# P in one two-head tile per fill, attention's output in six shared 4 KB tiles, X in three tiles

## The chip, the cores and the metric

The kernel runs on one core of one Trainium2 chip. The core has a matrix engine (TensorE, shown as PE, its weight loads as PEld), a vector engine (DVE), a scalar engine (ACT), GpSimd (POOL) and a queue engine (SP). They run side by side and wait for each other by semaphores. The metric is the device time of one execution in microseconds, and the median of several is compared. The profile calls the time from the first to the last instruction the span.

## The reference

One sequence of 2048 tokens with 640 features goes through two branches, and a gate mixes them. All is float32.

```python
def A(x):                                   # attention in 4 segments of 512 tokens, 32 heads of 20
    q, k, v = x @ wq, x @ wk, x @ wv        # each cut into heads and segments
    M, z = 0, 0
    for s in range(4):
        p = softmax(q[s] @ k[s].T * 20**-0.5 + causal_mask)
        a_dot = p @ v[s]
        a_mem = (phi(q[s]) @ M) / (phi(q[s]) @ z + 1e-6)   # phi(t) = t + 1 if t > 0 else exp(t)
        out[s] = g * a_mem + (1 - g) * a_dot               # g = sigmoid(beta), one per head
        M += phi(k[s]).T @ v[s];  z += phi(k[s]).sum()
    return out @ wo
def B(x): return (silu(x @ w1) * (x @ w3)) @ w2            # 1728 hidden features
gate = sigmoid((x * gate_w).sum(-1))
result = gate * A(x) + (1 - gate) * B(x)
```

## The kernel before

Features lie on the 128 partitions and tokens along the free dimension, so X of a segment is five blocks (kb 0 to 4) of 128 x 512. A factor of the large products is kept as a high and a low part (`split`, `split_psum`), and three passes (`PASSES`) are added in one PSUM bank: 15 matmuls of 512 columns make a block of 128 output features (`proj`). This makes q, k, the two FFN products g and u (all at L267), v (L398), the FFN's second product f (L593) and the output projection op (L852).

Attention runs in quads m of four heads (two pairs, k = 0 and 1, of two heads, i = 0 and 1). `s_fill` computes logits for the row maxima, which DVE takes (L654). `max_rows` turns the maxima round (tile `mr`) and sends them to two rows of the q tile `qk` by two transfers of ACT's queue (L670). `t_fill` then computes transposed logits in five fills of two banks, one bank for each i; a fill packs blocks (k, kb) at column o by the table `T_FILL`. ACT takes the exponential into P (L688), POOL zeroes what lies above the diagonal (`affine_select`, L693), and `pv_quad` multiplies P with V for four heads at once (L703). DVE copies the result to `oq`, from where it goes to DRAM as `od`. A visit to a quad stands at two places among the other matmuls: s0 t0 t1 o t3 s2 t2 s1 in the large one, s3 t4 s4 in the small one, where t and o belong to earlier quads (`VISITS`).

Three memories are of concern here. P is one tile of 2 x 1280 columns for a pair (10 KB in a partition; the table `PSEG` says where each kb lies), in three buffers that the first weights (`w01s`, `wr`) use too. `big_tile` is one buffer of 10.5 KB that holds in turn the raw weights `wr01`, the feature maps phi(q) of segments 1 and 2 (`pq`), the high part of segment 0's output (`oT`), X of segment 2 as loaded (`xr2`), and the memory's output `gm`. `oall` is one of 10 KB for attention's output as loaded from `od`, later its low part. The memory states `Ms` have ten tiles of 672 bytes. X has two buffers of 20 KB.

At a segment's end `o_load(c, b)` brings block b of attention's output from `od` (SP's queue, several pieces for a block), `load_memory(c)` the memory's output from `gd` (POOL's queue), and `normalize(c)` scales and adds both (rr, gt) and splits the sum for `oproj(c)`. For segment 1 `o_load` runs at about 610, 630 and 661 us, `load_memory` at 665 us, `normalize` at 690 us. `memory_read(2)`, the last to read `pq2`, ends at 664 us.

PE's instructions stand in the order in which the code writes them. The order on the other engines is made by the scheduler from its own estimate of times; `here` keeps an instruction in the written order. A transfer of SP or ACT takes one of eight semaphores (DMAHW0 to 7) in turn, and is not issued before the transfer that used the same semaphore last has landed; POOL's transfers do the same with eight of their own.

Of the kernel before, what the change touches and what calls it, by code (L numbers as in the profile page):

```python
# [17 lines left out]
P = 128  # L18
# [10 lines left out]
NP, AGE = 3, 4  # L29
# [5 lines left out]
PSEG = ((0, 512), (512, 384), (1024, 256), (896, 128))  # L35
# [3 lines left out]
def gated_mix(ctx: ExitStack, tc: tile.TileContext, xT, w01, wqk, wv, w13, w2, w2h, wo, beta, out):  # L39
# [27 lines left out]

    def constants():
# [6 lines left out]
        one = cp.tile([P, KB, L], F32, tag="oall", name="one", bufs=1)[:, 0]  # L75
# [75 lines left out]
    def big_tile(name, dt=F32):  # L151
        return sp.tile([P, 4 * H * VE], dt, tag="big", name=name, bufs=1)
# [10 lines left out]
    early, raws, clock = [], [], dict(step=0, oldest=2, next=2)  # L163

    def w_load():
        k = clock["next"]
        src, n, queue = items[k]
        if k in EARLY:
            if k % 2 == 0:
                early[:] = [sp.tile([P, 2, 1280], F32, tag="P32", name=f"wr{k}", bufs=NP)]  # L170
            raw = early[0][:, k % 2]
# [45 lines left out]
    def x_tile(c):  # L217
        Xs[c] = cp.tile([P, 2, KB, L], FR, tag="X", name=f"X{c}", bufs=2)

    def load_first(c):  # L220

        raw = big_tile("wr01")[:, :2 * D].rearrange("p (k n) -> p k n", k=KB)
        w01s.append(sp.tile([P, 2, KB, 2 * P], FR, tag="P32", name="w01s", bufs=NP))
        for kb in range(KB):
            r = xraw[c][:, kb]
            nc.sync.dma_start(r, xT[c, :, kb, :])
            nc.sync.dma_start(raw[:, kb], w01[kb])
            split(Xs[c][:, :, kb, :], r, lo=nc.vector.tensor_sub)
            split(w01s[0][:, :, kb], raw[:, kb], lo=nc.vector.tensor_sub)

    def load_wide(c):
# [4 lines left out]
        for kb in range(KB):  # L236
            split(Xs[c][:, :, kb, :], xraw[c][:, kb], lo=nc.vector.tensor_sub if kb % 2 else None)

    def load_raw(c):

        if c == 2:
            wide = big_tile(f"xr{c}")
            rs = [wide[:, kb * L:(kb + 1) * L] for kb in range(KB)]
# [9 lines left out]
    def split_x(c):  # L253
        x_tile(c)
        for kb in range(KB):
            split_psum(Xs[c][:, :, kb, :], xraw[c][kb], f"xh{c}_{kb}", here)
# [6 lines left out]
    def proj(ps, w, x):  # L263
        n = 0
        for kb in range(KB):
            for a, b in PASSES:
                nc.tensor.matmul(ps, w[:, a, kb * P:(kb + 1) * P], x[:, b, kb, :],  # L267
# [54 lines left out]
    def q_block(c, mb, i, alloc, oldest=None):  # L322
        ps = bank_tile(f"q{c}_{mb}", 1300)
        yield from proj(ps, w_get(i, oldest), Xs[c])
# [3 lines left out]
        s = parts(f"qs{c}_{mb}", ps, big["q", c][:, mb * L:(mb + 1) * L] if c else None)  # L328
# [3 lines left out]
    def q_blocks(c, mb, alloc):  # L332
        ps = [bank_tile(f"q{c}_{m}", 1300) for m in (mb, mb + 1)]
        n = 0
        for kb in range(KB):
            for a, b in ((0, 0), (1, 0), (0, 1)):
                for i in range(2):
                    nc.tensor.matmul(ps[i], w01s[0][:, a, kb, i * P:(i + 1) * P], Xs[c][:, b, kb, :],  # L338
# [7 lines left out]
        for i, m in enumerate((mb, mb + 1)):  # L346
            store_parts(0, c, m, parts(f"qs{c}_{m}", ps[i], big["q", c][:, m * L:(m + 1) * L] if c else None))
        yield 699

    def memory_read(c):  # L350
        pq = big.pop(("q", c))[:, :KB * L].rearrange("p (b n) -> p b n", b=KB)
        for qb in range(4):
            for hf in range(2):
# [10 lines left out]
                for n, (b, a0, u0, u1) in enumerate(todo):  # L364
                    nc.tensor.matmul(nd[:, u0 - 16 * hf:u1 - 16 * hf + 1, :],  # L365
                                     pq[:, b, qb * P:(qb + 1) * P],
# [11 lines left out]
    def v_blocks(c, iv, end):  # L378
        x = Xs[c]
# [6 lines left out]
        for lb in range(4):  # L386
# [5 lines left out]
            for hf in range(2):  # L392
# [3 lines left out]
                for kb in range(KB):  # L396
                    for a, b in PASSES:
                        nc.tensor.matmul(ps[:, :n1 - n0], x[:, a, kb, lb * P:(lb + 1) * P],  # L398
# [24 lines left out]
    def k_block(c, mb, i, prev):  # L423
# [4 lines left out]
        for n, y in enumerate(proj(ps, w_get(i), Xs[c])):  # L428
# [24 lines left out]
    def memory_write(c, mb):  # L453
# [18 lines left out]
        Ms[c, mb] = cp.tile([P, 8, VE], F32, tag=f"Ms{mb}", name=f"Ms{c}_{mb}", bufs=2)  # L472
# [47 lines left out]
    def ffn_up(cs, j, idx, oldest=None):  # L520
        half = j == NF
        for c in cs:
            shares_in = c != 1 and j in GROUPS[-1]
            ws = [w_get(i, idx[0] if oldest is None else oldest) for i in idx]
            x = Xs[c]
            pg = bank_tile(f"g{c}_{j}", 1300)
            yield from proj(pg, ws[0], x)
# [4 lines left out]
            if not half:  # L532
# [8 lines left out]
                yield from proj(pu, ws[1], x)  # L541
# [95 lines left out]
    T_FILL = (((0, 0, 0),), ((0, 1, 0), (0, 3, 384)), ((0, 2, 0), (1, 2, 256)), ((1, 0, 0),), ((1, 1, 0), (1, 3, 384)))  # L637
# [34 lines left out]
    def t_fill(m, f):  # L672

        todo = T_FILL[f]
        ps = [bank_tile(f"t{m}_{f}_{i}") for i in range(2)]
        for n, (k, kb, o) in enumerate(todo):
            u = pairs[2 * m + k]
            if "P" not in u:
                u["P"] = sp.tile([P, 2, 1280], F32, tag="P32", name=f"P{2 * m + k}", bufs=NP)
# [5 lines left out]
        outs = [(k, PSEG[kb][0], o, L if (kb, len(todo)) == (1, 2) else L - kb * P) for k, kb, o in todo if kb != 3]  # L685
        for i in range(2):
            for k, o, b, n in outs:
                last["exp"] = nc.scalar.activation(pairs[2 * m + k]["P"][:, i, o:o + n], ps[i][:, b:b + n],  # L688
                                                   AF.Exp, scale=SCALE)
                behind(last["exp"], "e")  # L690
        for k, o, n in (((0, 0, 1),), ((0, 512, 1),), ((0, 896, 2),), ((1, 0, 1),), ((1, 512, 1), (1, 896, 2)))[f]:
            d = pairs[2 * m + k]["P"][:, :, o:o + n * P].rearrange("p h (a b) -> p h a b", b=P)
            nc.gpsimd.affine_select(d, d, pattern=[[0, 2], [0, n], [1, P]], base=0, channel_multiplier=-1,  # L693
                                    compare_op=ALU.is_ge, fill=0.0)
# [3 lines left out]
    def pv_quad(p):  # L698

        ps = bank_tile(f"o{p}")  # L700
        for kb, (o, n) in enumerate(PSEG):
            for i in range(4):
                nc.tensor.matmul(ps[32 * i:32 * i + 32, kb * P:], heads[2 * p + i]["v"][:, kb],  # L703
                                 pairs[p + i // 2]["P"][:, i % 2, o:o + n],
# [6 lines left out]
        for b in OUT.get(q, ()):  # L711
            after(8, o_load, c, b)
# [29 lines left out]

# [354 lines left out]
```

## Time and profile before

| | |
|---|---|
| median of 3 executions | 1099.83 us (1099.75 to 1099.99) |
| profiled execution, span | 1098.7 us |
| what the timed executions have beyond that span | 1.1 us |
| granted TensorE clock | 1.00 |
| PE busy | 1093.1 us (99%), 6289 matmuls |
| PEld busy | 853.6 us (78%) |
| DVE, POOL, ACT busy | 603.1, 584.2, 381.9 us |

The page gives the profiled execution's span only, and no separate time of its own; the time around the span is therefore taken as the difference to the median. A line of the groups reads: source line, engine, operation, tiles written and read, how many; then busy time and the mean of one in ns; then the idle time of that engine just before them with what ended it. The matmuls are pipelined, so that the mean of one is longer than the step from one to the next. In the timeline a row starts with its start in us, then its duration.

### The profile page before, as it was taken

Reading aid. Unit: us, or ns where it says so; the run is one execution under the profiler, and the core shown is the slowest. Engines: PE = TensorE matmul, PEld = TensorE weight load, DVE = VectorE, ACT = ScalarE, POOL = GpSimd, SP = SyncE. Lnnn points to the kernel's source line nnn. Section 1 sums busy time; section 2 is a strip of 40 time slices with the busy share of each in tenths; the row PEclk is TensorE's granted clock in tenths of the full one; section 3 lists DMA queues with packets and bytes.
Section 4 is the critical chain, followed back from the end, with each engine's and each line's share of the span. In section 5 each row is a group of like instructions: output and inputs, shape, how many; then the busy total and the mean of one; then the engine's idle time right before and its main releaser. Section 6 shows DMA issues by size and latency. Waiting matters only on the chain.

```text
span 1098.7 us, 17910 instructions
## 1 busy us (share of the span) xinstructions
PE 1093.1 (99%) x6289; PEld 853.6 (78%) x6289; DVE 603.1 (55%) x1716; ACT 381.9 (35%) x829; POOL 584.2 (53%) x729
## 2 busy tenths in 40 slices
PE   9999999999999999999999999999999999999998
PEld 7988887777777777778977777777777777777787
DVE  6032474356555554566153678975657765551575
ACT  6244233443233122145244543424333332223020
POOL 5055556366366363566066447656674655565263
PEclk9999999999999999999999999999999999999999
DMA  9266943334355234435367966445664343432122
GB/s 314 105 207 222 284 123 82 95 83 117 77 141 124 58 85 124 137 83 184 112 201 264 298 216 185 112 148 140 161 149 111 96 113 97 111 102 89 52 79 96
DMA packets 87978, 153.21 MB, mean 139 GB/s; under 512 B 11632, under 2 KB 25872, under 8 KB 87888
## 3 DMA queue, kind: packets, MB, share of 16 engines
q1 hardware_dynamic: 63472, 106.30, 30.3%
q0 software_dynamic: 20384, 38.68, 15.6%
q10 hardware_dynamic: 4032, 7.08, 1.8%
q8 instruction: 50, 0.82, 0.3%
q14 instruction: 40, 0.33, 0.1%
HBM read 96.56 MB, written 54.54 MB: 138 GB/s over the span
## 4 chain that ended last, share of the span: by engine, by line
PE 99%; DMA 0%; ACT 0%; DVE 0%; SPq 0%; issue 0%
PE g L267 18%; PE f L593 18%; PE u L267 17%; PE o L703 7%; PE v L398 7%; PE op L852 6%; PE k L267 6%; PE q L267 5%; PE s L647 5%; PE t L682 4%; PE nd L365 2%; PE pm L462 1%; PE q L338 1%; PE gt L783 1%; PE pkt L447 1%; PE rr L777 0%
## 5 line engine op out<-in xcount | busy, mean ns | idle before, releaser
L654 DVE CUSTOM_DVE_ANT_0 junk<-s,mask 128x256 bf16<-128x256 f32 (+3 forms) x512 | 250.4, 489 | 106.1 <-PE s L647 74.0
L688 ACT ACTIVATE P<-t 128x512 f32<-128x512 f32 (+1 forms) x384 | 172.5, 536 | 187.7 <-PE t L682 145.1
L267 PE MATMUL g<-X,W 128*128 128x512 f32 x840 | 208.9, 398 | 0.1
L190 POOL TENSOR_TENSOR W<-wr,W 128x640 fp32r<-128x640 f32 (+1 forms) x126 | 198.8, 1583 | 2.5
L267 PE MATMUL u<-X,W 128*128 128x512 f32 x780 | 196.9, 399 | 0.0
L593 PE MATMUL f<-ht,W 128*128 128x512 f32 (+1 forms) x825 | 196.4, 395 | 0.0
L185 POOL CAST W<-wr 128x640 fp32r<-128x640 f32 (+1 forms) x126 | 92.6, 739 | 195.1 <-PE v L398 44.6
L693 POOL TENSOR_SCALAR_AFFINE_SELECT P<-P 128x256 f32<-128x256 f32 x192 | 93.6, 497 | 179.5 <-ACT P L688 179.2
L267 PEld LDWEIGHTS g<-X,W 128*128 128x128 f32 x840 | 155.8, 188 | 37.3 <-DVE m L654 0.4
L593 PEld LDWEIGHTS f<-ht,W 128*128 128x128 f32 x825 | 153.1, 188 | 36.3
L267 PEld LDWEIGHTS u<-X,W 128*128 128x128 f32 x780 | 144.0, 188 | 34.5 <-ACT P L688 0.3
L117 POOL TENSOR_TENSOR ht<-ft,ht 128x512 fp32r<-128x512 f32 x52 | 67.5, 1298 | 91.1 <-ACT ht L116 91.0
L624 POOL DMA_DIRECT2D qk<-qkd x128 | 83.3, 652 | 0.5 <-issue 0.2
L647 PE MATMUL s<-qk 60*128 60x256 f32 (+3 forms) x512 | 77.7, 346 | 0.0
L267 PE MATMUL k<-X,W 128*128 128x512 f32 x300 | 77.2, 404 | 0.0
L703 PE MATMUL o<-P,vg 128*32 128x512 f32 (+3 forms) x1024 | 75.5, 435 | 0.1
L533 ACT ACTIVATE ft<-g 128x512 f32<-128x512 f32 x52 | 31.2, 600 | 126.5 <-PE g L267 113.8
L534 DVE SCALAR_TENSOR_TENSOR fu<-ft,g 128x512 f32<-128x512 f32 x52 | 35.6, 685 | 67.9 <-ACT ft L533 58.8
L398 PE MATMUL v<-W,X 128*128 128x320 f32 (+1 forms) x480 | 72.1, 311 | 0.2 <-ACT P L688 0.2
L398 PEld LDWEIGHTS v<-W,X 128*128 128x128 f32 x480 | 71.2, 189 | 0.9 <-ACT P L688 0.4
L116 ACT CAST ht<-ft 128x512 fp32r<-128x512 f32 x52 | 32.2, 619 | 109.9 <-DVE ft L542 108.1
L601 DVE TENSOR_TENSOR acc<-f,acc 128x512 f32<-128x512 f32 x65 | 44.8, 689 | 39.5 <-PE f L593 39.2
(125 smaller groups left out, 1209.3 us busy)
## 6 DMA issues: line engine op xcount, KB each, us to landing
qk<-qkd POOLq DMA_DIRECT2D x128, 240.0 KB, 4.1
wr<-in_w_dram SPq DMA_DIRECT2D x80, 320.0 KB
qkd<-qs SPq DMA_DIRECT2D x20, 512.0 KB
qkd<-ks SPq DMA_DIRECT2D x20, 512.0 KB
od<-oq SPq DMA_DIRECT2D x32, 256.0 KB
wr<-in_wo_dram SPq DMA_DIRECT2D x20, 320.0 KB
vg<-vd SPq DMA_DIRECT2D x16, 336.0 KB
xr<-in_xT_dram SPq DMA_DIRECT2D x20, 256.0 KB
```

The costliest lines, as they stand in the source:

```text
L117: (lo or nc.gpsimd.tensor_sub)(dst[:, 1], src, dst[:, 0].bitcast(F32))
L185: hi = nc.gpsimd.tensor_copy(w[:, 0, :n], raw[:, :n])
L190: last["low"] = nc.gpsimd.tensor_sub(w[:, 1, :n], raw[:, :n], w[:, 0, :n].bitcast(F32))
L267: nc.tensor.matmul(ps, w[:, a, kb * P:(kb + 1) * P], x[:, b, kb, :], start=n == 0, stop=n == 14)
L398: nc.tensor.matmul(ps[:, :n1 - n0], x[:, a, kb, lb * P:(lb + 1) * P], wvt[kb][:, b, n0:n1], start=n == 0, stop=n == 14)
L593: nc.tensor.matmul(ps[:, :n1 - n0], w, h, start=n == 0, stop=n == len(ms) - 1)
L624: here(nc.gpsimd.dma_start(t[64 * i:64 * i + RH], qkd[c][RH * (h + i):RH * (h + i + 1)]))
L647: nc.tensor.matmul(ps[i][:, o:o + w], q[:, qb * P:(qb + 1) * P], key[:, :w], start=n == 0, stop=n == len(todo) - 1, skip_group_check=True)
L654: r = nc.vector.tensor_tensor_reduce(out=junk[:, :w], in0=ps[i][:, o:o + w], in1=mask[:, L - w:], scale=1.0, scalar=-3.0e38, op0=ALU.add, ...
L688: last["exp"] = nc.scalar.activation(pairs[2 * m + k]["P"][:, i, o:o + n], ps[i][:, b:b + n], AF.Exp, scale=SCALE)
L693: nc.gpsimd.affine_select(d, d, pattern=[[0, 2], [0, n], [1, P]], base=0, channel_multiplier=-1, compare_op=ALU.is_ge, fill=0.0)
L703: nc.tensor.matmul(ps[32 * i:32 * i + 32, kb * P:], heads[2 * p + i]["v"][:, kb], pairs[p + i // 2]["P"][:, i % 2, o:o + n], start=kb == 0 ...
```

## The change

- P: `t_fill` takes one tile of 2 x 512 columns (4 KB, seven buffers) for a fill. The tile holds what the two banks hold, so ACT writes one 512-column exponential for each bank. Fill 2, which holds blocks of both pairs, had four of 256 columns. `T_FILL` puts kb 3 ahead of kb 1 in fills 1 and 4, so that one `affine_select` per fill covers all diagonal blocks: five for a quad instead of six.
- Six tiles of 4 KB (`r_tile`, tag R) replace `big`, `oall` and most of `Ms`: the constant `one`, `wr01`, `pq1`, `pq2`, `xr2`, the states after segments 0 and 2, and one tile `N` for each block of a segment's output, which holds the memory's output (then the high part) beside attention's output (then the low part).
- `load_memory` makes five transfers, one for a block, instead of four, one for a quarter of the tokens. For segment 1 `o_load` of blocks 0 to 3 moves there.
- X of a segment lies in three tiles (kb 0 and 1, 2 and 3, 4).

```diff
+NP, NR, AGE = 7, 6, 4
-PSEG = ((0, 512), (512, 384), (1024, 256), (896, 128))
...
+    def r_tile(name, dt=F32):
+        return cp.tile([P, 2, L], dt, tag="R", name=name, bufs=NR)
+    def p_tile(name, dt=F32):
+        return sp.tile([P, 2, L], dt, tag="P", name=name, bufs=NP)
...
-        Xs[c] = cp.tile([P, 2, KB, L], FR, tag="X", name=f"X{c}", bufs=2)
+        Xs[c] = [cp.tile([P, 2, n, L], FR, tag=f"X{t}", name=f"X{t}{c}", bufs=2) for t, n in (("A", 2), ("B", 2), ("E", 1))]
...
-    T_FILL = (((0, 0, 0),), ((0, 1, 0), (0, 3, 384)), ((0, 2, 0), (1, 2, 256)), ((1, 0, 0),), ((1, 1, 0), (1, 3, 384)))
+    T_FILL = (((0, 0, 0),), ((0, 1, 128), (0, 3, 0)), ((0, 2, 0), (1, 2, 256)), ((1, 0, 0),), ((1, 1, 128), (1, 3, 0)))
...
     def t_fill(m, f):
+        pt = p_tile(f"P{m}_{f}")
...
-            for k, o, b, n in outs:
-                last["exp"] = nc.scalar.activation(pairs[2 * m + k]["P"][:, i, o:o + n], ps[i][:, b:b + n],
-                                                   AF.Exp, scale=SCALE)
+            last["exp"] = nc.scalar.activation(pt[:, i], ps[i], AF.Exp, scale=SCALE)
...
         for b in OUT.get(q, ()):
-            after(8, o_load, c, b)
+            if c != 1:
+                after(8, o_load, c, b)
...
+    def n_tile(c, b):
+        if (c, b) not in oall:
+            oall[c, b] = r_tile(f"N{c}_{b}", FR)
+        return oall[c, b]
...
     def load_memory(c):
-        gms[c] = big_tile(f"gm{c}", FR)[:, :KB * L].rearrange("p (b n) -> p b n", b=KB)
-        for qb in range(4):
-            here(nc.gpsimd.dma_start(gms[c].bitcast(F32)[:, :, qb * P:(qb + 1) * P],
-                                     gd[c][:, qb].rearrange("p (b n) -> p b n", b=KB)))
+        for b in range(KB):
+            here(nc.gpsimd.dma_start(n_tile(c, b)[:, 0].bitcast(F32).rearrange("p (a n) -> p a n", n=P),
+                                     gd[c][:, :, b * P:(b + 1) * P]))
+            if c == 1 and b < KB - 1:
+                o_load(c, b)
             yield 1
```

PE's 5645 instructions and DVE's 1716 stand in the same order as before, each with the same shape. The order of the other engines changes at the places below.

ACT, the large and the small visit to quad 16 (pairs 32 and 33; in a name t16_2_0 the quad, the fill and i). Before, from fill 3 on:

```order
L688 ACTIVATE P33_6829<-t16_3_0_6827 128x512
L688 ACTIVATE P33_6829<-t16_3_1_6828 128x512
L688 ACTIVATE P32_6792<-t16_2_0_6843 128x256
L688 ACTIVATE P33_6829<-t16_2_0_6843 128x256
L688 ACTIVATE P32_6792<-t16_2_1_6844 128x256
L688 ACTIVATE P33_6829<-t16_2_1_6844 128x256
L688 ACTIVATE P33_6829<-t16_4_0_6918 128x512
```

and now, where the two numbers behind a P are the quad and the fill:

```order
L704 ACTIVATE P16_3_6832<-t16_3_0_6833 128x512
L704 ACTIVATE P16_3_6832<-t16_3_1_6834 128x512
L704 ACTIVATE P16_2_6848<-t16_2_0_6849 128x512
L704 ACTIVATE P16_2_6848<-t16_2_1_6850 128x512
L704 ACTIVATE P16_4_6927<-t16_4_0_6928 128x512
```

Fill 2 has two exponentials in place of four; the rest stands as it did.

SP's queue, between 653 and 676 us of the profile before (quad 15's output goes out, segment 1's output comes in; in brackets the semaphores that an instruction waits for). Before, blocks 0 to 3 of segment 1 have been loaded some 20 to 50 us earlier, and here stand:

```order
L627 DMA vg1_93<-vd2_74 128x4x168 [waits DMAHW7_49,PE_49]
L720 DMA rs_97<-od1_77 128x1x128 [waits DMAHW6_49,DMAHW0_49]
L722 DMA er1_6873<-ed1_85 128x1x128 [waits DMAHW1_49]
L286 DMA gd2_82<-gm2_2_1_6875 128x320 [waits DMAHW2_49,DVE_49]
L752 DMA oall1_6272<-od1_77 8x512 [waits DMAHW3_49]
L750 DMA oall1_6272<-od1_77 120x1x512 [waits DMAHW4_49]
L286 DMA gd2_82<-gm2_3_0_6895 128x320 [waits DMAHW5_49,DVE_49]
L286 DMA gd2_82<-gm2_3_1_6961 128x320 [waits DVE_49]
```

and now, with nine transfers more between `er` and the next weights (two of block 0 stand ahead of `vg`, and behind these rows one of block 2 and three of block 3):

```order
L301 DMA gd2_82<-gm2_2_1_6879 128x320 [waits DMAHW1_49,DVE_49]
L777 DMA N1_1_6893<-od1_77 12x512 [waits DMAHW2_49]
L775 DMA N1_1_6893<-od1_77 100x1x512 [waits DMAHW3_49]
L777 DMA N1_1_6893<-od1_77 16x512 [waits DMAHW4_49]
L777 DMA N1_4_6901<-od1_77 8x512 [waits PE_49]
L775 DMA N1_4_6901<-od1_77 120x1x512 [waits DMAHW6_49]
L301 DMA gd2_82<-gm2_3_0_6904 128x320 [waits DMAHW7_49,DVE_49]
L777 DMA N1_2_6966<-od1_77 4x512 [waits DMAHW0_49,PE_49]
L775 DMA N1_2_6966<-od1_77 120x1x512 [waits DMAHW1_49]
```

Three pieces here wait for PE, which reads `pq2` in the memory that they take over. The long piece of block 4 uses DMAHW6, the first of block 2 DMAHW0.

ACT's queue a little later, before:

```order
L533 ACTIVATE ft3_0_6974<-g3_0_6884 128x512 [waits PE_49,Pool_49]
L141 CAST ns1_101<-m68_6545 128x16 [waits DVE_49]
L142 COPY nh34_6948<-ns1_101 128x16 [waits Activation_49]
L670 DMA qk1_91<-mr_6952 2x8x128 [waits DMAHW7_49,DVE_49]
L670 DMA qk1_91<-mr_6952 2x8x128 [waits DMAHW0_49]
L116 CAST ht3_0_6973<-ft3_0_6974 128x512 [waits DVE_49]
```

and now:

```order
L551 ACTIVATE ft3_0_6987<-g3_0_6888 128x512 [waits PE_49,Pool_49]
L146 CAST ns1_101<-m68_6553 128x16 [waits DVE_49]
L147 COPY nh34_6957<-ns1_101 128x16 [waits Activation_49]
L688 DMA qk1_91<-mr_6961 2x8x128 [waits DMAHW6_49,DVE_49]
L688 DMA qk1_91<-mr_6961 2x8x128 [waits DMAHW0_49]
L121 CAST ht3_0_6986<-ft3_0_6987 128x512 [waits DMAHW7_49,DVE_49]
```

The two transfers of `mr` stand where they stood. They used to wait for `vg` and `rs`; they now wait for the long piece of N1_4 and the first of N1_2.

POOL's queue at the same time: the four transfers of `gm` stood together behind the selects of quad 16 and ahead of weights 83 and 84. Now N1_0's stands ahead of these selects, N1_1's among them, N1_2's and N1_3's behind them, and N1_4's between weights 83 and 84.

More of the change, by code (lines that the diff above doesn't have):

```diff
@@ L74, in constants @@
             nc.gpsimd.memset(v[:, :, VG:], 0.0)
-        one = cp.tile([P, KB, L], F32, tag="oall", name="one", bufs=1)[:, 0]
+        one = r_tile("one")[:, 0]
         nc.gpsimd.memset(one, -1.0)
@@ L149, in slot, with rows_of, rows_in_slot @@
         return cp.tile([P, 4 * H * VE], F32, tag="acc", name=name, bufs=2)
-    def big_tile(name, dt=F32):
-        return sp.tile([P, 4 * H * VE], dt, tag="big", name=name, bufs=1)
+    def rows_of(name, n=KB):
+        ts = [r_tile(f"{name}_{i}") for i in range((n + 1) // 2)]
+        return [ts[i // 2][:, i % 2] for i in range(n)]
+    def rows_in_slot(name):
+        t = slot(name)
+        return [t[:, i * L:(i + 1) * L] for i in range(KB)]
     def f_tile(name):
@@ L236, in load_wide @@
         for kb in range(KB):
-            split(Xs[c][:, :, kb, :], xraw[c][:, kb], lo=nc.vector.tensor_sub if kb % 2 else None)
+            split(xb(c, kb), xraw[c][:, kb], lo=nc.vector.tensor_sub if kb % 2 else None)
     def load_raw(c):
         if c == 2:
-            wide = big_tile(f"xr{c}")
-            rs = [wide[:, kb * L:(kb + 1) * L] for kb in range(KB)]
+            rs = rows_of(f"xr{c}")
         else:
@@ L337, in q_blocks @@
                 for i in range(2):
[L338 removed]
+                    nc.tensor.matmul(ps[i], w01s[kb][:, a, i * P:(i + 1) * P], xs(c, b, kb),
                                      start=kb == a == b == 0, stop=(kb, b) == (KB - 1, 1))
@@ L851, in rest @@
                     for a, b in PASSES:
-                        nc.tensor.matmul(ps, ws[kb][:, b, fb * P:(fb + 1) * P], oT[a][:, kb], start=n == 0, stop=n == 14)
+                        nc.tensor.matmul(ps, ws[kb][:, b, fb * P:(fb + 1) * P], n_tile(c, kb)[:, a], start=n == 0, stop=n == 14)
                         n += 1
```

103 lines of the change are left out of this document (53 added, 50 removed).

## The prediction

> **What bounds the kernel now.** I read the page's busy times and its chain first, then four stretches of the span, then what PE and its weight loads wait for.
>
> ```profile
> span 1098.7 us, 17910 instructions
> PE 1093.1 (99%) x6289; PEld 853.6 (78%) x6289; DVE 603.1 (55%) x1716; ACT 381.9 (35%) x829; POOL 584.2 (53%) x729
> PE 99%; DMA 0%; ACT 0%; DVE 0%; SPq 0%; issue 0%
> ```
>
> PE is busy for all but 5.6 us of the span, and the chain that ended last runs through it for 99%. Where those 5.6 us lie is seen in stretches (length, then PE's busy time first, then PEld's):
>
> ```profile
> 0.00:8.00 8.00, 6.45 (x17) 2.62 (x18) 2.92 (x6) 3.96 (x7) 4.72 (x15) 1.00 0.71 211
> 8.00:125.00 117.00, 116.97 (x647) 102.96 (x648) 36.17 (x55) 49.35 (x110) 52.69 (x75) 1.00 0.64 218
> 125.00:1083.00 958.00, 957.57 (x5572) 738.11 (x5571) 555.71 (x1644) 328.58 (x714) 526.11 (x640) 1.00 0.46 129
> 1083.00:1098.70 15.70, 12.12 (x58) 9.89 (x56) 8.27 (x13) 0.00 (x0) 0.72 (x1) 0.97 0.44 169
> ```
>
> PE idles 1.55 us at the start, 3.58 us at the end, and 0.03 + 0.43 = 0.46 us in the 1075 us between, where nearly all of the change lies. The waits of PE itself are these, in the whole run:
>
> ```profile
> PE warm L921 <- DVE zero L918: 1.3, 1, 1.3
> PE q L338 <- ACT w01s L116: 0.2, 1, 0.2
> PE v L398 <- ACT P L688: 0.2, 1, 0.2
> ```
>
> A matmul's end is modelled, so a short wait can hide under a predecessor's tail. The weight loads in front of the matmuls show more:
>
> ```profile
> L267 PEld LDWEIGHTS g<-X,W 128*128 128x128 f32 x840 | 155.8, 188 | 37.3 <-DVE m L654 0.4
> L267 PEld LDWEIGHTS u<-X,W 128*128 128x128 f32 x780 | 144.0, 188 | 34.5 <-ACT P L688 0.3 <-issue 0.2
> L398 PEld LDWEIGHTS v<-W,X 128*128 128x128 f32 x480 | 71.2, 189 | 0.9 <-ACT P L688 0.4 <-DVE W L117 0.3
> L783 PEld LDWEIGHTS gt<-ident,gm 128*128 128x128 f32 x60 | 7.5, 141 | 1.4 <-ACT P L688 0.3
> ```
>
> Waits for an exponential add up to 0.3 + 0.4 + 0.3 = 1.0 us. That is all that a faster ACT could give back to PE.
>
> **The change, part by part.** PE's and DVE's instructions keep order and shape, so their own time changes by nothing; only waits can move it.
>
> *Exponentials and selects.* In each of 32 quads, four 256-column exponentials become two of 512, and six selects five: fills 1 and 4 now take four blocks each, of which fill 1 had two, and fill 4's separate select of two blocks goes.
>
> ```profile
> L688 ACT ACTIVATE P<-t 128x512 f32<-128x512 f32 x256 | 137.0, 600 | 187.5 <-PE t L682 144.9 <-DVE acc L601 18.9 <-DVE acc L564 12.9
> L688 ACT ACTIVATE P<-t 128x256 f32<-128x256 f32 x128 | 39.1, 409 | 0.2 <-PE t L682 0.2
> L693 POOL TENSOR_SCALAR_AFFINE_SELECT P<-P 128x256 f32<-128x256 f32 x128 | 53.8, 423 | 170.7 <-ACT P L688 170.4
> L693 POOL TENSOR_SCALAR_AFFINE_SELECT P<-P 128x512 f32<-128x512 f32 x64 | 41.2, 643 | 8.8 <-ACT P L688 8.8
> ```
>
> Instructions on ACT overlap, so I take busy time over count: 39.1/128 = 0.305 us and 137.0/256 = 0.535 us. ACT saves 32 x (4 x 0.305 - 2 x 0.535) = 4.8 us. POOL goes from 53.8 + 41.2 = 95.0 us to 64 x 0.420 + 96 x 0.644 = 88.7 us and saves 6.3 us. Both engines sit idle ahead of these rows (187.5 and 170.7 us), so neither saving is on the path. Bounds for the total: no gain, or the whole 1.0 us of waits for exponentials. I take 0, because fill 2 stands behind fill 3 in the visit, and a PE that waits within the visit waits for the earlier of the two.
>
> *P's buffers.* Seven tiles of 4 KB leave two spare when a quad's five are in use; the fills t0 and t1 need just two before o of the previous quad frees five. That is the same point at which the third 10 KB buffer was taken before. Price 0, by PE's order: o stands ahead of t3 and t2 on PE, and their exponentials wait for t3 and t2 anyway.
>
> *Six R tiles and X in three.* No instruction is added on PE, DVE or ACT. Segment 0's blocks are loaded when they were; xr2 gets two tiles earlier than it had `big`. A split of X starts when ACT's and DVE's order says, which has not changed. Price 0.
>
> *load_memory.* Three segments make five transfers instead of four on POOL.
>
> ```profile
> L765 POOL DMA_DIRECT2D gm<-gd x12 | 10.8, 903 | 0.0
> 664.96 3.54 POOL L765 DMA_DIRECT2D gm<-gd x4
> qk<-qkd POOLq DMA_DIRECT2D x128, 240.0 KB, 4.1
> ```
>
> Each has 512 pieces of 512 bytes instead of 640, the total being the same. POOL pays between 0 (cost by pieces) and 3 x 0.9 = 2.7 us (cost by transfer) in all. Weights 83 and 84 wait behind them on POOL, but they serve `oproj(1)`, after 690 us. Price 0.
>
> *Segment 1's output loaded late.* This is the part that adds waits. Eleven of the thirteen pieces of attention's output move from 610 to 639 us to behind 653 us, into this stretch:
>
> ```profile
> 660.07 0.59 SPq L722 DMA_DIRECT2D er<-ed  x1
> 660.92 0.38 SPq L286 DMA_DIRECT2D gd<-gm  x1
> 661.35 0.32 SPq L752 DMA_DIRECT2D oall<-od  x1
> 661.73 0.77 SPq L750 DMA_DIRECT2D oall<-od  x1
> 667.63 1.08 ACTq L670 DMA_DIRECT2D qk<-mr  x2
> 669.11 0.62 ACT L116 CAST ht<-ft 128x512 fp32r<-128x512 f32 x1 [3.07 <-DVE ft L542]
> 675.56 0.64 PE L682 MATMUL t<-qk 62*128 62x512 f32 x6
> ```
>
> On SP, three pieces of N1_1 (0.32 + 0.77 + 0.32) follow the store that ends at 661.3, then a short one of N1_4 (0.32), so N1_4's long piece is issued at about 663.1 and N1_2's first at about 664.3. ACT's two transfers of mr now wait for those two to land; before, they waited for older ones and left at 667.63. Behind them on ACT stand the cast at 669.11 and later work with slack; on PE, t at 675.56 needs both rows. The profile has no landing times for SP's and ACT's own transfers, so I bound them by POOL's in the same stretch (median us to landing, last column):
>
> ```profile
> gm<-gd POOLq DMA_DIRECT2D x4, 320.0 KB, 7.1
> qk<-qkd POOLq DMA_DIRECT2D x4, 240.0 KB, 5.3
> oall<-od SPq DMA_DIRECT2D x1, 240.0 KB
> ```
>
> and by 4.1 us, the median for qk over the whole run (above). N1_4 lands between 663.1 + 4.1 = 667.2 and 663.1 + 7.1 = 670.2. If the second transfer of mr starts 0.54 us behind the first, it leaves between 668.2 (as before) and 670.7, and lands between 672.3 and 677.8. Against 675.56 PE waits between 0 and 2.2 us. If N1_2's first piece is itself held by `er` (issued 660.07, landed by 667.2), mr's second leaves at up to 667.2 + 7.1 = 674.3 at the worst, and PE waits up to 5.8 us. With 5.3 us for each step (the piece of the same 240 KB): 663.1 + 5.3 + 0.54 + 5.3 = 674.2, no wait. Since these steps lie near the edge, I take 0.4 us.
>
> The bytes do not pile up: of gm's 1.3 MB, two fifths now leave earlier and one fifth later, against 0.8 MB of N1 pieces that come in. Nor is N1 itself late: it has landed by about 675 us, and `normalize` reads it from here on:
>
> ```profile
> L778 DVE TENSOR_TENSOR on<-oall,rr x3: 680/687/689, 689.9 to 695.4; 128x512 f32<-128x512 f32 x3
> ```
>
> [...]
>
> **Sum.** Start and end unchanged, exponentials 0, P, R and X 0, POOL 0, mr +0.4: the span goes from 1098.7 to 1099.1 us. With 1.13 us around the span (1099.83 - 1098.7), the median goes from 1099.83 to 1100.2 us.
>
> **Rivals.**
> - *Slower by more than 0.2%* (2.2 us, about what a measurement of this kernel can tell from no change): PE's t at 675.56 waits for mr. It decides when mr's second transfer lands after 677.8, which takes steps of 7.1 us and more, or N1_2 held by `er`. The worst case above gives 1099.8 + 5.8 = 1105.6, the typical one 2.2 to 3, so 1102.5 us. For it: `gm` took 7.1 us there. Against it: mr itself is 8 KB and got through before 675.56 from 668.17.
> - *Faster by more than 0.2%*: PE is not full, and smaller tiles and fewer instructions fill hidden bubbles. The page's PEld at 78% leaves 245 us. A dense row contradicts it:
>
> ```profile
> 1045.21 10.44 PE g L267 x45
> ```
>
> A step of 10.44/45 = 232 ns with a load of 188 ns is 81% for PEld at its densest, so 78% is nearly full; named waits for ACT give 1.0 us at most. The rival needs another 1.2 us that no row names; it would give some 1097 us. [...]
> - *The change does not do what it says*: the pieces of N1_0 and N1_1 find their tiles late, or `normalize` waits. They have 14 us of room at 690 us, so this too ends at 1099.8.
>
> **How the numbers follow.** No measurable change, by the sum or with any wait below 2.2 us: 0.86. Slower by the mr rival: 0.10. Faster: 0.04. The range goes from the whole 1.0 us of ACT's waits gained (1098.8) to the end of the bounded wait without `er` (1099.8 + 2.2, and a little of the rival above it: 1102.4).
>
> **What would show it.** Right: PE busy within 1 us of 1093.1, 320 exponentials with some 171 us busy, 160 selects with some 89 us, mr's transfers near 668 to 671 us at the place above, t there at 675.5 to 677 us. Wrong: a PE or PEld row that waits for DMA qk or for N, idle PE of more than 3 us between 125 and 1083 us, or a dense step away from 232 ns.

## The result, and the profile after

The changed kernel takes 1107.22 us (1106.51 to 1108.18, 4 runs) against 1099.79 us: a ratio of 1.0067, interval [1.0053, 1.0081]. It is 7.4 us slower. I had given this side 0.10, with 1102.5 to 1105.6 us; the time lies above my range and above the worst case.

The page of the changed kernel (span, busy times, the start of the chain that ended last) and PE's own waits:

```profile
span 1106.4 us, 17912 instructions
PE 1095.7 (99%) x6289; PEld 855.7 (77%) x6289; DVE 600.8 (54%) x1716; ACT 377.5 (34%) x765; POOL 577.8 (52%) x700
PE 97%; DMA 2%; ACT 0%; DVE 0%; SPq 0%; issue 0%; ACTq 0%
```

```profile
PE t L700 <- DMA qk<-mr: 4.6, 1, 4.6
PE warm L942 <- DVE zero L939: 1.3, 1, 1.3
```

A DMA stands in the chain now. At the start q waits 0.7 us longer for its first weights than before, but at 22 us PE is level with the kernel before again. Behind the start there is one new wait: t for mr, where the rival had put it. Stretches of the changed kernel around it (length; busy time of PE, PEld, DVE, ACT, POOL; granted clock; DMA share, that is the time of all packets over that of 16 engines, which can pass 1; GB/s):

```profile
125.00:661.00 536.00, 535.62 (x3096) 419.41 (x3094) 293.33 (x884) 191.47 (x387) 276.99 (x334) 1.00 0.48 140
671.00:676.00 5.00, 5.00 (x23) 3.72 (x21) 1.82 (x6) 0.00 (x0) 0.00 (x0) 1.00 0.53 153
676.00:681.00 5.00, 0.41 (x4) 0.22 (x4) 2.27 (x5) 1.11 (x2) 3.09 (x3) 0.87 0.25 91
681.00:686.00 5.00, 5.00 (x34) 2.06 (x38) 0.41 (x2) 2.57 (x5) 4.15 (x5) 0.50 0.68 204
691.00:1091.00 400.00, 399.97 (x2339) 302.74 (x2339) 244.28 (x704) 125.03 (x247) 228.20 (x259) 1.00 0.41 108
```

PE stands still from 676 to 681 us, and in the five microseconds behind it runs at half clock. Everywhere else it is as full as before. PE's timeline of both kernels gives the sum; first the changed one:

```profile
675.72 0.50 PE L665 MATMUL s<-qk 60*128 60x512 f32 x2
680.81 1.22 PE L700 MATMUL t<-qk 62*128 62x512 f32 x6 [4.59 <-DMA qk<-mr]
681.96 4.49 PE L724 MATMUL o<-P,vg 128*32 128x512 f32 x32
687.71 1.65 PE L282 MATMUL g<-XA,W 128*128 128x512 f32 x6
```

and before, where s stood at 675.22 and t at 675.56:

```profile
676.12 2.36 PE L703 MATMUL o<-P,vg 128*32 128x512 f32 x32
679.72 3.77 PE L267 MATMUL g<-X,W 128*128 128x512 f32 x15
```

The s in front is 0.50 us behind, t 5.25, the g after the visit 7.99. So 4.75 us come from the wait and 2.74 from the clock: o took 4.49 instead of 2.36, the six t 1.22 instead of 0.64. Together these are 7.5 of the 7.7 us between the spans. The profiled execution is the slowest of the four (1108.18 us).

Why mr was late is seen on SP's and ACT's queues (changed kernel, timeline):

```profile
662.71 0.39 SPq L777 DMA_DIRECT2D N<-od  x1
663.15 0.81 SPq L775 DMA_DIRECT2D N<-od  x1
664.00 0.81 SPq L777 DMA_DIRECT2D N<-od  x2
664.86 0.77 SPq L775 DMA_DIRECT2D N<-od  x1
665.73 0.41 SPq L301 DMA_DIRECT2D gd<-gm  x1
666.78 0.25 SPq L777 DMA_DIRECT2D N<-od  x1
```

```profile
676.03 1.08 ACTq L688 DMA_DIRECT2D qk<-mr  x2
677.21 0.62 ACT L121 CAST ht<-ft 128x512 fp32r<-128x512 f32 x1 [10.70 <-DMA qk<-mr]
```

N1_4's long piece is issued at 664.86. The trace's semaphore updates (the source of every landing time below) have it landed at 675.96, and N1_2's first at 676.37. ACT's first transfer of mr leaves at 676.03, its second behind 676.37; they land at 680.55 and 680.72, and t starts at 680.81. Before, N1_4's counterpart took from 661.73 to 668.70, and mr had landed by 674.25.

A second wait lies hidden under this one (changed kernel, DVE's timeline):

```profile
678.50 0.69 DVE L552 SCALAR_TENSOR_TENSOR fu<-ft,g 128x512 f32<-128x512 f32 x1 [5.50 <-DMA gd<-gm]
```

The last store of `memory_read(2)`'s result, gd<-gm, now stands behind the pieces on SP's queue and lands at 678.40 (before: 672.48). The tile gm came from the same four `f` buffers as fu, so DVE must wait for it; o then takes over the PSUM bank that fu reads. By this row (fu ends at 679.19), I estimate that o would have stood at some 679 us instead of 676 without any wait for mr; in e3 below, where mr is free, it stood at 677.55.

The rest of the change did as forecast: 320 exponentials, 160 selects, and no wait of PE for them beyond the 0.2 us at v of before (changed kernel, groups):

```profile
L704 ACT ACTIVATE P<-t 128x512 f32<-128x512 f32 x320 | 168.4, 602 | 192.1 <-PE t L700 190.7
L713 POOL TENSOR_SCALAR_AFFINE_SELECT P<-P 128x512 f32<-128x512 f32 (+1 forms) x160 | 87.8, 553 | 179.1 <-ACT P L704 174.9
```

### The profile page after: what moved, and what is told of

It is laid out like the page before. It is cut to its first block, busy times and chain, and to the rows that moved or that the text cites. A ratio compares the mean times of both kernels' runs of the same rounds, so it can differ in the third digit from the quotient of the medians.

```text
span 1106.4 us, 17912 instructions
## 1 busy us (share of the span) xinstructions
PE 1095.7 (99%) x6289; PEld 855.7 (77%) x6289; DVE 600.8 (54%) x1716; ACT 377.5 (34%) x765; POOL 577.8 (52%) x700
## 4 chain that ended last, share of the span: by engine, by line
PE 97%; DMA 2%; ACT 0%; DVE 0%; SPq 0%; issue 0%; ACTq 0%
PE g L282 18%; PE f L611 17%; PE u L282 16%; PE o L724 7%; PE v L412 6%; PE op L873 6%; PE k L282 6%; PE q L282 5%; PE s L665 5%; PE t L700 4%; PE nd L380 2%; PE pm L476 1%; PE q L353 1%; DMA N<-od 1%; PE gt L805 1%; PE pkt L461 1%
## 5 line engine op out<-in xcount | busy, mean ns | idle before, releaser
L704 ACT ACTIVATE P<-t 128x512 f32<-128x512 f32 x320 | 168.4, 602 | 192.1 <-PE t L700 190.7
L713 POOL TENSOR_SCALAR_AFFINE_SELECT P<-P 128x512 f32<-128x512 f32 (+1 forms) x160 | 87.8, 553 | 179.1 <-ACT P L704 174.9
L282 PE MATMUL g<-XA,W 128*128 128x512 f32 x336 | 88.7, 399 | 0.1
L282 PE MATMUL g<-XB,W 128*128 128x512 f32 x336 | 88.5, 398 | 0.0
L282 PE MATMUL u<-XB,W 128*128 128x512 f32 x312 | 83.7, 400 | 0.0
L282 PE MATMUL u<-XA,W 128*128 128x512 f32 x312 | 83.3, 401 | 0.0
L282 PEld LDWEIGHTS g<-XB,W 128*128 128x128 f32 x336 | 62.4, 188 | 14.8
L282 PEld LDWEIGHTS g<-XA,W 128*128 128x128 f32 x336 | 62.3, 188 | 15.0 <-DVE m L672 0.4
L873 PE MATMUL op<-N,W 128*128 128x512 f32 x300 | 72.7, 398 | 0.0
L121 ACT CAST ht<-ft 128x512 fp32r<-128x512 f32 x52 | 32.2, 619 | 118.4 <-DVE ft L560 107.6
L282 PEld LDWEIGHTS u<-XB,W 128*128 128x128 f32 x312 | 57.5, 188 | 14.0 <-issue 0.2
```

Of the source, the lines that this page charges most:

```text
L282: nc.tensor.matmul(ps, w[:, a, kb * P:(kb + 1) * P], xs(c, b, kb), start=n == 0, stop=n == 14)
L704: last["exp"] = nc.scalar.activation(pt[:, i], ps[i], AF.Exp, scale=SCALE)
L713: nc.gpsimd.affine_select(d, d, pattern=pattern, base=0, channel_multiplier=-1, compare_op=ALU.is_ge, fill=0.0)
L873: nc.tensor.matmul(ps, ws[kb][:, b, fb * P:(fb + 1) * P], n_tile(c, kb)[:, a], start=n == 0, stop=n == 14)
```

## The experiments

| run | kernel | median us | ratio to before, interval | PE waits near 676 us |
|---|---|---|---|---|
| - | the change | 1107.22 | 1.0067 [1.0053, 1.0081] | t 4.6 |
| e1 | before + late loads | 1106.17 | 1.0059 [1.0044, 1.0074] | t 3.9 |
| e2 | before + P | 1099.71 | 0.9999 [0.9989, 1.0009] | none |
| e3 | change, mr by POOL | 1103.95 | 1.0039 [1.0025, 1.0052] | o 1.6 |
| e4 | change, loads behind mr | 1100.97 | 1.0013 [1.0003, 1.0022] | o 0.25 |
| e5 | change, 5 f buffers | 1106.97 | 1.0065 [1.0050, 1.0080] | t 3.9 |
| e6 | e3, 5 f buffers | 1102.05 | 1.0022 [1.0013, 1.0032] | o 0.9 |
| e7 | e4, 5 f buffers | 1100.69 | 1.0008 [0.9998, 1.0017] | o 0.2 |
| e8 | change, block 3 behind mr | 1103.24 | 1.0033 [1.0019, 1.0046] | t 1.3, o 0.4 |
| e9 | e7, o_scale later | 1100.55 | 1.0010 [1.0000, 1.0019] | none |
| e10 | e6, o_scale later | 1102.26 | 1.0025 [1.0016, 1.0035] | none |
| e11 | change, 240 KB more (DRAM) | 1107.14 | 1.0070 [1.0055, 1.0085] | t 4.7 |
| e12 | before + P, X, load_memory | 1100.08 | 1.0003 [0.9993, 1.0012] | o 0.3 |
| e13 | change, memory's loads later | 1100.73 | 1.0008 [0.9999, 1.0018] | t 0.2 |
| e14 | change, 240 KB more (SBUF) | 1107.95 | 1.0071 [1.0054, 1.0088] | t 5.7 |

**Which part costs: e1, e2, e12.** The late loads alone, in the kernel before:

```diff
         for b in OUT.get(q, ()):
-            after(8, o_load, c, b)
+            if c != 1:
+                after(8, o_load, c, b)
...
             here(nc.gpsimd.dma_start(gms[c].bitcast(F32)[:, :, qb * P:(qb + 1) * P], ...))
+            if c == 1:
+                o_load(c, qb)
             yield 1
```

> The kernel before, with one part of the change: the eleven pieces of segment 1's attention output (blocks 0 to 3) are loaded inside load_memory(1); P, X, big and oall stay as before. Theory A (mr's two transfers are held on ACT's queue by the late pieces through the shared semaphores, and the clock falls behind the idle time): the whole loss returns, 1105.5 to 1108.5 us, with 3.5 to 5.5 us of waiting at t for qk<-mr near 676 us and a granted clock near 0.5 in the 5 us behind it. Rival B (P's tiles, the X tiles or the shared R tiles cause the loss): 1099.5 to 1100.5 us and no such wait.

1106.17 us. PE's timeline of e1, and its stretch behind:

```profile
679.89 1.22 PE L682 MATMUL t<-qk 62*128 62x512 f32 x6 [3.94 <-DMA qk<-mr]
681.00:686.00 5.00, 5.00 (x39) 1.87 (x38) 1.10 (x3) 2.27 (x5) 2.02 (x3) 0.53 0.35 90
```

The same wait and the same half clock. P alone is the kernel before with the change's `t_fill`, `pv_quad` and p_tile, `big`, `oall` and all loads as they were:

```diff
+        pt = p_tile(f"P{m}_{f}")
...
-            if "P" not in u:
-                u["P"] = sp.tile([P, 2, 1280], F32, tag="P32", name=f"P{2 * m + k}", bufs=NP)
+            u["P", kb] = pt, o
...
+            last["exp"] = nc.scalar.activation(pt[:, i], ps[i], AF.Exp, scale=SCALE)
```

> The kernel before, with another part alone: P in 4 KB tiles of a fill, T_FILL's new columns, 320 exponentials and 160 selects; big, oall, X and all loads as before. Theory A: 1099.3 to 1100.3 us, ACT near 377 us busy and POOL near 578 us, t at 675 to 676 us with no wait. Rival B: 1101 us or more, with PE waits for exponentials, selects or P's buffers.

1099.71 us; nothing moves. With X in three tiles and this besides:

```diff
-        for qb in range(4):
-            here(nc.gpsimd.dma_start(gms[c].bitcast(F32)[:, :, qb * P:(qb + 1) * P], ...))
+        for b in range(KB):
+            here(nc.gpsimd.dma_start(gms[c][:, b].bitcast(F32).rearrange("p (a n) -> p a n", n=P),
+                                     gd[c][:, :, b * P:(b + 1) * P]))
```

> The kernel before with P in tiles of a fill and the new fills (as in e2_P_alone), X in three tiles, and load_memory in five transfers, one for a block; big, oall and Ms stay, and segment 1's output is loaded at 610 to 661 us as before. Theory A (the move of the loads is the only part that costs): 1099.3 to 1100.4 us, mr leaves at 667 to 669 us, no wait of PE near 676 us. Rival G (the rest of e9's excess of 1 us comes from these parts): 1100.5 to 1101.5 us.

1100.08 us, no difference that this can measure. So the move makes the loss, 6.5 of the 7.4 us by itself (e1).

**By which way the pieces reach mr: e3, e5, e6, e8.** In e3 mr of that one quad goes by POOL's queue, which shares no semaphore with SP:

```diff
-            after(4, lambda d=dst, r=16 * a: here(nc.scalar.dma_start(d, mr[r:r + 16])))
+            e = nc.gpsimd if p == 34 else nc.scalar
+            after(4, lambda d=dst, r=16 * a, e=e: here(e.dma_start(d, mr[r:r + 16])))
```

> The changed kernel, but the two transfers of mr for the quad of pairs 34 and 35 go by POOL's queue, which has semaphores of its own; all loads of N stay. Theory A: mr leaves near 670 us, t waits less than 1 us, 1099.8 to 1101 us. Rival C (the DMA engines are full there, and mr would be late whatever it waits for): mr lands near 680 us all the same, t waits 4 us or more, 1106 to 1108 us.

The wait for mr is gone, as theory A said, but the time is 1103.95 us, 3 us above its bound. The profiled execution was the fastest of the five and shows what took its place, fu's wait for gd (DVE) and then o's (PE):

```profile
676.76 0.69 DVE L552 SCALAR_TENSOR_TENSOR fu<-ft,g 128x512 f32<-128x512 f32 x1 [0.61 <-DMA gd<-gm]
677.55 2.36 PE L725 MATMUL o<-P,vg 128*32 128x512 f32 x32 [1.62 <-issue]
```

o's wait is called "issue", since the profile names no releaser; its own semaphores name fu, which ended 0.1 us ahead. This is the hidden second wait. It is not all of the 3 us: the two executions with a mean granted clock of 1.00 took 1101.74 and 1102.87 us, the three with 0.998 took 1103.95, 1105.13 and 1105.54 us. A mean of 0.998 is what e8's profiled execution has with its 3.4 us at half clock (below), so the clock most likely fell in these three as well; they have no trace that shows how long PE stood still. A fifth f buffer takes fu's wait for the store away; e5 is the change with this alone, e6 has e3's edit too:

```diff
-        return sp.tile([P, L], F32, tag="f", name=name, bufs=4)
+        return sp.tile([P, L], F32, tag="f", name=name, bufs=5)
```

> The changed kernel with a fifth buffer of f tiles (4 before). After the first runs theory A has a second wait: the late pieces also hold the last store of memory_read(2) (gm to gd) on SP's queue, its f tile is wanted by fu2_1 on DVE, and PE's o waits for the bank that fu2_1 reads. Theory A: with mr still held, the wait for mr alone gives the whole loss, 1106 to 1108 us, t waiting 4 to 5 us. Rival D (the f buffer is the cause and mr only its companion): below 1102 us.

> The changed kernel with mr of pairs 34 and 35 on POOL's queue (as in e3_mr_by_POOL, 1103.95 us) and a fifth f buffer, all late loads in place. Theory A: both waits are gone, o of quad 16 at 675.5 to 676.5 us follows t without a wait of over 0.5 us, 1099.6 to 1101 us. Rival C (the full DMA engines themselves delay PE): the time stays above 1102.5 us, with a wait for another transfer.

e5 stays at 1106.97 us: with mr held, the f buffer makes no difference. e6 falls to 1102.05 us from 1103.95, which lies between what the two theories allowed (up to 1101, from 1102.5 on); o still waits 0.9 us for fu, which no transfer holds any more. In e8 mr stays on ACT, and only block 3's three pieces go behind it, which changes mr's partners in the semaphores:

```diff
-            if c == 1 and b < KB - 1:
+            if c == 1 and b < KB - 2:
                 o_load(c, b)
+            if c == 1 and b == KB - 1:
+                after(4, o_load, c, KB - 2)
```

> The changed kernel, in which only block 3's three pieces are loaded later, behind mr. All that stands ahead of mr on SP's queue stays; but mr's two transfers now share their semaphores with the last piece of N1_1 and the first of N1_4, which landed at 670.4 and 670.6 us, in place of N1_4's long piece (675.8) and N1_2's first (676.2). Theory A: mr leaves at 669.5 to 671 us, t waits less than 1 us; the last store of gm is still behind the pieces, so o of quad 16 waits 1 to 3.5 us for fu2_1: 1101 to 1105 us. Rival C: mr lands as late as before (near 680 us), 1106 to 1108 us.

```profile
669.94 1.08 ACTq L688 DMA_DIRECT2D qk<-mr  x2
```

mr leaves at 669.94 instead of 676.03, just behind the landing of its new partners (669.86 and 670.29). Nothing that stands ahead of it on SP had moved. So the shared semaphore held it, not the traffic by itself. t waits 1.3 us, a little more than expected, and 1103.24 us lies within.

**Loads out of the way: e4, e7, e9, e10.** In e4 and e7 blocks 0 to 3 come after the five transfers of the memory's output; e7 has the fifth f buffer too.

```diff
-            if c == 1 and b < KB - 1:
-                o_load(c, b)
             yield 1
+        if c == 1:
+            for b in range(KB - 1):
+                o_load(c, b)
+                yield 1
```

> The changed kernel, with blocks 0 to 3 of segment 1's output loaded by load_memory(1) after all five transfers of the memory's output, so that they stand behind mr and the weights wr85 and the rR rows on SP's queue. Theory A: mr leaves near 668 us, t stands at 675 to 676.5 us without a wait, 1099.6 to 1100.8 us, if N1 has landed when normalize reads it (near 690 us). Rival C: the same traffic some us later, so a wait of 1 us or more appears at N or at the weights near 690 us, above 1101.5 us.

> The changed kernel with blocks 0 to 3 loaded behind mr (as in e4_loads_behind_mr, 1100.97 us) and a fifth f buffer. Theory A: the 0.3 us at o of quad 16 go, 1099.5 to 1100.4 us. Rival E (the rest of e4's excess comes from N landing late for normalize): no change, 1100.6 to 1101.6 us.

1100.97 and 1100.69 us. 6.3 to 6.5 of the 7.4 us are back, with the rest of the change in place; e4 is just above what A allowed. e7 lies in the range of rival E, not of A, though its o waits 0.2 us as before; the step from e4 to e7 is too small to say. e9 and e10 put DVE's work on rs and rp behind fu:

```diff
-        after(22 if c < NSEG - 1 else 3, o_scale, c, er)
+        after(30 if c == 1 else 22 if c < NSEG - 1 else 3, o_scale, c, er)
```

> As e7_loads_behind_f_buffer (1100.69 us), and for segment 1 o_scale is called 30 slots behind o_sums in place of 22, which puts fu2_1 ahead of the four slow operations on rs and rp on DVE. Theory F (what is left of the loss is this chain on DVE, which POOL's work on weights slows, so that fu2_1 and with it the bank of o come late): 1099.4 to 1100.3 us, o of quad 16 follows t without a wait. Rival E (N or the weights land late near 690 us): 1100.5 to 1101.5 us as before.

> As e6_mr_by_POOL_f_buffer (1102.05 us), with o_scale of segment 1 at 30 slots as well; all late loads stay where the change put them. Theory F: o of quad 16 waits no more, 1099.5 to 1100.9 us. Rival C (the full DMA engines delay PE in some other way): 1101.5 us or more.

In both profiles o follows t without a wait, yet the times do not fall: 1100.55 and 1102.26 us, in the ranges of rivals E and C. Theory F explains the last wait at o but not the last microsecond. What is left is 1.0 us in e9 and 2.7 us in e10 against the kernel before on the same chip.

Half a microsecond of it stands long before 676 us. PE runs the same 6289 matmuls in the same order in every version, so their starts can be compared one by one. From the s at 125.82 us to the q at 633.10 us PE takes 507.28 us in the kernel before, and 507.19, 507.28 and 507.35 us in e1, e2 and e12. In the change and in all that is built on it PE takes 507.60 to 507.81 us (e9: 507.79, e10: 507.77). The difference comes in steps of about 0.1 us at most, mostly far smaller. These versions have the shared R tiles, and e1, e2 and e12 do not; no run has the R tiles alone, and how they would cost PE time is open. In e10's profile s waits 0.3 us more behind o, and the last store lands 2.7 us after its issue instead of 1.9. The rest is not settled. Rival E looked for it near 690 us, but in e9's trace PE loses nothing against the kernel before from 676 to 858 us.

**What made the pieces land late: e11, e14, e13.** e11 puts 240 KB more ahead on SP's queue, from DRAM to DRAM; e14 the same into a spare SBUF tile, in the form of N1_4's piece (shown):

```diff
+            if c == 1 and b == 1:
+                here(nc.sync.dma_start(spare[:120], od[c][:6, :DH]))
             if c == 1 and b < KB - 1:
                 o_load(c, b)
```

> The changed kernel with one transfer more on SP's queue ahead of N1_1's pieces: 240 KB from od to a spare place in DRAM, which nobody reads. The second transfer of mr now shares its semaphore with the store of gm that stands behind N1_4's long piece. Theory A: all that stands behind lands later by the time of those bytes, 4 to 7 us; t waits 8 to 12 us for mr in place of 4.6, the clock is at 0.5 for 1.7 to 3.4 us' worth of loss as before: 1110.5 to 1115 us. Rival B or D (the late pieces are not what mr waits for): 1106 to 1108.5 us.

> The changed kernel with one transfer more on SP's queue ahead of N1_1's pieces: 240 KB from od to a spare tile in SBUF, in 120 rows as N1_4's long piece, which nobody reads. Theory I: what stands behind lands 3 us or more later, t waits 7.5 to 11 us, 1109 to 1113.5 us. Theory H: as in e11_more_bytes_ahead, less than 1.5 us later, 1106.5 to 1108.5 us.

1107.14 and 1107.95 us. N1_4's long piece landed at 676.58 and 676.66, only 0.6 to 0.7 us later than in the changed kernel, or 1.1 and 0.9 us later if counted from the same q of PE (at 633.48 us in the changed kernel, 632.99 in e11, 633.29 in e14). e11's expectation was over 3 us too high: 240 KB more on the piece's own queue explain little of its 11.1 us. Nor does t wait for this piece here: mr's first transfer leaves at 672.96 and 672.93, and the second shares its semaphore with the store of gm behind N1_4, which lands at 677.00 and 677.08. So the two runs bear on the landing, and not on t. (e11 has a second wait, 0.7 us at an earlier o at 655 us.) e13 leaves SP and ACT alone and moves POOL's five transfers of the memory's output behind W83 and W84:

```diff
+        def bring(b):
+            here(nc.gpsimd.dma_start(n_tile(c, b)[:, 0]..., gd[c][:, :, b * P:(b + 1) * P]))
         for b in range(KB):
-            here(nc.gpsimd.dma_start(n_tile(c, b)[:, 0]..., gd[c][:, :, b * P:(b + 1) * P]))
-            if c == 1 and b < KB - 1:
+            n_tile(c, b)
+            if c != 1:
+                bring(b)
+            elif b < KB - 1:
                 o_load(c, b)
+            else:
+                for b in range(KB):
+                    after(8, bring, b)
             yield 1
```

> The changed kernel; the five transfers of the memory's output of segment 1 on POOL's queue stand behind the weights W83 and W84 instead of between 650 and 681 us among quad 16's selects. SP's and ACT's queues and their semaphores stay as in the changed kernel. Theory H (POOL's transfers hold SP's pieces back, the DMA engines being shared): N1_4's long piece lands 3 us or more earlier, near 672 us, t waits for mr less than 2 us, 1100.5 to 1104 us. Theory I (SP's pieces wait for each other alone): no change, t waits 4 to 5 us, 1106 to 1108 us.

1100.73 us. Its timelines (SP, ACT, PE, POOL):

```profile
663.08 0.77 SPq L775 DMA_DIRECT2D N<-od  x1
670.28 1.09 ACTq L688 DMA_DIRECT2D qk<-mr  x2
675.54 0.73 PE L700 MATMUL t<-qk 62*128 62x512 f32 x6 [0.23 <-DMA qk<-mr]
674.92 3.79 POOL L787 DMA_DIRECT2D N<-gd  x5
```

N1_4's long piece, still in its place and with the same semaphores, is issued at 663.08 and lands at 670.20: 7.1 us instead of 11.1. It was issued 1.8 us earlier; 0.9 us of this is a shift of the whole profile (PE's s at 661.24 us in the changed kernel stands at 660.34), and by the rest the queue itself moved faster. The DMA engines from 661 to 671 us, in the kernel before, the changed kernel and e13:

```profile
661.00:671.00 10.00, 10.00 (x55) 8.28 (x54) 8.71 (x33) 2.69 (x6) 8.27 (x11) 1.00 1.01 264
661.00:671.00 10.00, 10.00 (x57) 8.27 (x56) 7.82 (x33) 2.06 (x5) 6.24 (x9) 1.00 1.15 247
661.00:671.00 10.00, 10.00 (x53) 8.16 (x50) 8.60 (x34) 2.06 (x5) 4.87 (x6) 1.00 0.79 221
```

The change moves fewer bytes there than the kernel before (247 against 264 GB/s) and keeps the engines busy longer for them (1.15 against 1.01). So POOL's transfers of gd, in 512-byte pieces, hold SP's pieces back, and this is what let the shared semaphore reach PE. It goes the other way too: POOL's transfers for N1_2 and N1_3 take 9.1 and 9.5 us to land in the changed kernel, and 6.6 and 6.9 us in e4, where SP's pieces come later. Since e13 changes one place of the program alone, it is also the plainest repair. It is no faster than the kernel before, and neither is any other version here.

One thing in the traces that no run tests: as N1_4's long piece lands, its semaphore is updated six times (671.55 to 675.96 us), while vg, 336 KB on the same queue and issued 6.6 us earlier, has sixteen updates and lands after 5.1 us. What an update stands for, and whether the long pieces would land sooner if cut in another way, is open.

## Why the prediction was wrong

- *The path.* That the pieces of N1_4 and N1_2 hold mr on ACT's queue, and mr holds t, was right (e8, e3), and its price was the only cost in my sum. The case with `er` came true as well: N1_2's first piece left at 666.78, behind er's landing at 666.72, and landed at 676.37, so that each of the two would have held mr by itself. Named with 0.10, it should have been the first case: my own bounds for mr's landing, 672.3 to 677.8 us, lay on both sides of the 675.56 at which t needs it.
- *The step that failed: "N1_4 lands between 663.1 + 4.1 and 663.1 + 7.1".* It was issued at 664.86 (0.5 us of the difference is a shift of the whole profile) and took 11.1 us; the term for mr, put at +0.4 us, measured 4.75 us of waiting and 2.7 us of clock behind it. I had taken landing times from POOL's rows of the kernel before and used the largest as an upper bound. That was the time in the old mixture; the change itself put SP's pieces beside POOL's transfers, and e13 shows what they do to each other: 7.1 us apart, 11.1 together. My sentence "the bytes do not pile up" counted bytes, which were not the measure (the rows above, and e11 and e14). mr's own flight, 4.5 us, was within what I took.
- *The term that was missing.* I priced a wait at its length. The 4.75 us lie inside the 5.8 us of my worst case; it is the clock that put the time above 1105.6 us. PE's clock was at half speed (granted 0.50) for 6.83 us from 679.75 us on, and this added 2.7 us to the 4.75. The stretches that I quoted showed the clock fall, 1.00 everywhere and 0.97 at the end, where PE idles for 3.58 us; I did not ask what the same would do in the middle.
- *The wait that I did not see.* gm's store, f buffers, fu, the bank of o. The order showed the store waiting for its turn behind N1_2 on SP; I followed the queue only to mr. It costs nothing here, under mr, and 1.9 us as soon as mr is free (1103.95 us in e3 against 1102.05 in e6).
- *Right.* P, the exponentials and selects, X, five transfers: 0 was taken, e2 and e12 measure 0.0 and +0.4 us with intervals on both sides of 1. By the rows of the exponentials ACT saved 137.0 + 39.1 - 168.4 = 7.7 us, by its whole busy time 381.9 - 377.5 = 4.4 us, near my 4.8, and none of it reached PE. The rival with hidden bubbles on PE did not show: PE's busy share is as before. The 0 for the R tiles is not measured by itself; 0.3 to 0.5 us between 126 and 633 us speak against it. (The 1.13 us that I took around the span compares two executions; an execution of these runs is mostly 1.7 to 1.8 us longer than its own span. It stands on both sides and changes no difference.)
- *ACT behind mr.* ACT stood still with its transfers of mr: the cast that stands behind them (ht, L121) came at 677.21 us after 10.70 us of idle, before at 669.11 after 3.07. I had counted on slack there, and in the profile PE does not wait for it.

## What to carry to other kernels

When a transfer moves, list for eight transfers behind it who takes the same semaphore next, and for each tile that its queue's later stores free, who waits for the tile; then ask for the slack of the matmul at the end. Take the time to landing not from the old schedule but as unknown upwards wherever the move brings two queues of small pieces together: N1_4's long piece took 11.1 us beside POOL's transfers, and 7.1 with these out of the way (e13). On a PE that is full, price a wait of some microseconds at its length plus what the half clock behind it adds: in the changed kernel 4.75 us became 7.5, with 6.83 us at 0.50; in e3's profile no half clock followed 1.62 us.

## What the runs showed of the hardware

The record of the granted clock tells something of how much idle it took for the clock to fall. In the changed kernel PE paused for 4.6 us, up to 680.81 us, and the clock was at 0.50 for 6.83 us from 679.75 us on. In e1 and e14, with one pause of 3.9 and 5.7 us, it was 0.78 and 0.74 from 676 to 681 us and 0.53 and 0.58 from 681 to 686 us; if it was either 1.00 or 0.50, as in the changed kernel, I estimate some 6.9 and 6.8 us at 0.50 from this. In e5 and e11, with 3.9 and 4.7 us, the mean of the whole profiled execution was 0.997 and 0.996 (the changed kernel: 0.997). With one pause of 1.62 us (e3) it stayed at 1.00 in each stretch from 671 to 691 us, and with 0.89 us (e6) the mean was 0.999. But e8, with pauses of 1.27 and 0.40 us close together, was at 0.80 and 0.86 in the two stretches, by the same estimate some 3.4 us at 0.50:

```profile
678.30 3.84 PE L724 MATMUL o<-P,vg 128*32 128x512 f32 x32 [0.40 <-issue]
676.00:681.00 5.00, 3.43 (x27) 1.72 (x31) 2.68 (x6) 2.59 (x5) 2.29 (x3) 0.80 0.74 224
681.00:686.00 5.00, 4.97 (x39) 3.68 (x32) 3.23 (x10) 2.17 (x5) 2.43 (x5) 0.86 0.25 91
```

No pause of e8 is as long as the 1.62 us of e3, yet the clock fell in e8's profile and not in e3's. So the length of the longest pause alone did not decide it. How much idle it takes, e3 and e8 alone do not tell: e8's two pauses add up to 1.67 us, hardly more than e3's 1.62, and three other executions of e3 had a mean clock of 0.998.

DVE's short operations on rs and rp took longer beside POOL's work on ht and the weights: 1.34 and 1.48 us in the kernel before, with that work beside them (second and third operation of DVE's chain, and POOL's timeline), and 0.35 and 0.23 us in the changed one, with POOL idle from 671 to 676 us:

```profile
669.97 1.34 DVE L732 SCALAR_TENSOR_TENSOR rs<-rs,cR,er 128x128 f32<-128x128 f32 x1
671.34 1.48 DVE L733 CAST rp<-rs 128x128 bf16<-128x128 f32 x1
669.85 1.29 POOL L117 TENSOR_TENSOR ht<-ft,ht 128x512 fp32r<-128x512 f32 x1
671.11 3.16 POOL L190 TENSOR_TENSOR W<-wr,W 128x640 fp32r<-128x640 f32 x2
```

```profile
671.47 0.35 DVE L754 SCALAR_TENSOR_TENSOR rs<-rs,cR,er 128x128 f32<-128x128 f32 x1
671.86 0.23 DVE L755 CAST rp<-rs 128x128 bf16<-128x128 f32 x1
```

In e3 the first of them took 2.68 us (from 669.69), and POOL was busy for 4.39 of the 5 us from 671 us on; in e6 it took 2.71 us. The chain then kept fu until 676.68 in e6, and this is why o still waited 0.9 us there; with the chain behind fu, in e10, this wait is gone.
